# Keys, queries, values and sinks handed to a fused attention and two-layer MLP kernel in the layout of its groups

## The chip, the core and the metric

The kernel runs on one core of a Trainium2 chip. The metric is the device time of one execution in microseconds (us), as a median of several runs; lower is better. In the core, TensorE (PE) does the matrix products and the transposes into PSUM, ScalarE (ACT) and VectorE (DVE) read PSUM and do the elementwise work, GpSimd (POOL) does elementwise work on SBUF, and SyncE (SP) issues nearly all transfers. Each engine carries out its own instructions in a fixed order and waits on semaphores for the others.

## What is computed

Attention with two batches, eight heads, 768 positions and 64 channels per head, in which a query sees the first `n_sink` (4) keys and a window of 128 keys; then, on the 1536 x 512 result, two MLP layers. All weights come as 64-bit floats.

```python
scores = scale * np.matmul(q, k.transpose(0, 1, 3, 2))
keep = is_sink | in_window
scores = np.where(keep, scores, -1000000000.0)
a = np.exp(scores - np.max(scores, axis=-1, keepdims=True))
a = a / (np.sum(a, axis=-1, keepdims=True) + 1e-09)
attn = np.matmul(a, v)
...
g = x @ w_gate
y = (g * (1.0 / (1.0 + np.exp(-g))) * (x @ w_val)) @ w_out
h = y @ w_in
out = (np.maximum(h, 0.0) + alpha * np.minimum(h, 0.0)) @ w_out2
```

## The kernel before

The attention is cut into 24 groups. A group is one batch, one pair of heads (`hp`, of four) and 256 queries (two blocks of 128, from block `i0` on). The first eight groups have `i0 == 0`; they have no separate sink keys. The sixteen others (`i0` 2 or 4) see one key block before their own two and 32 sink keys; they come in pairs of neighbours, and the second of a pair (`before` is set) takes its first key block from the first one.

A score product contracts over the 64 channels of a head, so keys and queries must lie with channels on the partitions: two heads of 64 channels fill the 128 partitions. The inputs have positions on the rows. Therefore `load` (line 172) brings keys (`kr`) and queries (`qr`) with positions on the partitions, in runs of one head's 64 channels (256 bytes). `prep` (line 214) turns them: four transposes on TensorE into one PSUM tile `ps_k` (line 230) and a copy of it on ScalarE into the tile `th` (line 233 or 235); for the first of a pair one more transpose and copy (lines 225 and 226); for the second of a pair a copy on GpSimd (line 222); and for both a copy of the sink keys on GpSimd (line 219), which `sink_keys` (line 371) made by one transpose and one copy for each batch (lines 373 and 374). `load_v` brings values (`vr`), and for `i0 == 2` the sink values (`vsr`, line 209), four small transfers into a tile that GpSimd set to zero once (line 138).

`attention` (line 387) is the pipeline: in turn x it does the scores of group x, the values of group x - 3, the flips of group x - 2, the norm of group x, the prep of group x + 2, and it issues the loads of group x + 3 and the values of group x + 1. `scores` makes four score tiles `ps_s` (line 266), DVE adds the mask and takes the row's maximum (line 272, for sink groups after a merge in line 270), ACT takes the exponential with the row sum (line 276). `norm` makes the reciprocals `rinv` on DVE and scales on POOL. `flip` transposes the probabilities (line 321) and brings them to SBUF as `pt` (ACT in line 325 for the first eight groups, DVE in line 327 for the others). `values` makes `xp` (lines 352 and 357), and `put` splits it into a high part `xh` (ACT, line 869) and a low part `xl` (DVE, line 870).

Beside it the weights are streamed: a slice `w_raw` of 512 KB is loaded (lines 567 and 569), ACT makes `w_m` from it (line 585), DVE does three bit operations (lines 601, 604 and 607), ACT rounds to `wh` (line 615) and DVE makes the rest `wl` (line 621). The first 12 slices serve the first step (unit 0) of the MLP for all three passes of 512 positions, and they fill the 12 places that there are. After eight groups the attention is interleaved with the unit for the first pass, after sixteen with that for the second: each `yield` of the pipeline adds to `cost` (440 of it for each prep, 3,600 for the other parts of a group), and whenever `cost` has reached `WEAVE` = 2300 one step of the MLP is put in, and one step of a weight's conversion. What `cost` was gathered in the first eight groups is spent right after them.

The order on DVE is that of the code. On the other engines and queues a scheduler orders the instructions, by its own estimate of times. All PSUM tiles come from one pool of eight (`ps`).

Of the kernel before, what the change touches and what calls it, by code (L numbers as in the profile page):

```python
# [44 lines left out]
KW = P + SINK  # L45
DOWN = float(2.0**-112)
# [84 lines left out]
def attention_pools(nc, tc, ctx, g):  # L131
    for nm, bufs in (("raw_p", 2), ("tr_p", 3), ("pr_p", 3), ("pt_p", 2), ("st_p", 4)):
        setattr(g, nm, ctx.enter_context(tc.tile_pool(name=nm, bufs=bufs)))
    g.nb = g.const.tile([P, B * H * NQ], F32, name="nb")
    g.wsum = g.const.tile([P, NW], F32, name="wsum")
    g.kst = [g.const.tile([P, NPAIR * SINK], F32, name="kst") for _ in range(B)]
    g.vsr = g.const.tile([4 * SINK, NPAIR, NG, 2 * D], F32, name="vsr")
    nc.gpsimd.memset(g.vsr, 0.0)


class Group:
    def __init__(self, nc, g, q, k, v, b, hp, i0, put, cs, blk):
        self.nc, self.g, self.q, self.k, self.v = nc, g, q, k, v
# [7 lines left out]
        self.before = self.lead = None  # L151
        if self.sink:
            self.kpos = [0, P, P + KW]
            self.spos = 2 * P
            self.qpos = [P + 2 * KW, P + 3 * KW]
        else:
            self.kpos = [0, P]
            self.qpos = [2 * P, 3 * P]

    def wide(self, src, tag, bufs):  # L160
        t = self.g.raw_p.tile([P, NG, 4, D], F32, tag=tag, name=tag, bufs=bufs)
        for x in range(NG):
            self.nc.sync.dma_start(
                out=t[:, x], in_=src[self.b, self.h0:self.h0 + 4, x * P:(x + 1) * P, :].rearrange("h p d -> p h d")
            )
        return t

    def pair(self, t):
        e = 0 if self.lead is None else 2
        return t[:, :, e:e + 2].rearrange("p t e d -> p t (e d)")  # L170

    def load(self):
        nc, p = self.nc, self.g.raw_p
        b, h0, i0 = self.b, self.h0, self.i0
        if i0 == 0:
            if self.lead is None:
                self.raw = [self.wide(self.k, "kr", 2), self.wide(self.q, "qr", 2)]
            else:
                self.raw = self.lead.raw
            self.kr, self.qr = (self.pair(t) for t in self.raw)  # L180
            return
        n0 = 1 if self.before is not None else 0
        j0, nk = self.j0 + n0, self.nk - n0
        kr = p.tile([P, NG, 4, D], F32, tag="kr", name="kr", bufs=2)
        qr = p.tile([P, NG, 4, D], F32, tag="qr", name="qr", bufs=2)
        kr, qr = (x.rearrange("p t h d -> p (t h d)") for x in (kr, qr))
        kr = kr[:, :NK * 2 * D].rearrange("p (t e d) -> p t e d", e=2, d=D)
        qr = qr[:, :NG * 2 * D].rearrange("p (t e d) -> p t e d", e=2, d=D)
# [3 lines left out]
        self.qr, self.kr = (x.rearrange("p t e d -> p t (e d)") for x in (qr, kr))  # L192

    def load_v(self):
        nc, p = self.nc, self.g.raw_p
        b, h0, j0, nk = self.b, self.h0, self.j0, self.nk
        if self.i0 == 0:
            self.vt = self.wide(self.v, "vr", VB) if self.lead is None else self.lead.vt
            o = 0 if self.lead is None else 2
            self.vr = [[self.vt[:, t, o + e] for e in range(2)] for t in range(nk)]  # L200
            return
        vr = p.tile([P, NG, 4, D], F32, tag="vr", name="vr", bufs=VB).rearrange("p t h d -> p (t h d)")
        vr = vr[:, :NK * 2 * D].rearrange("p (t e d) -> p t e d", e=2, d=D)
        for e in range(2):
            nc.sync.dma_start(out=vr[:, :nk, e], in_=self.v[b, h0 + e, j0 * P:(j0 + nk) * P, :].rearrange("(t p) d -> p t d", p=P))
            if self.i0 == NG:
                for t in range(NG):
                    r = (2 * t + e) * SINK
                    nc.sync.dma_start(
                        out=self.g.vsr[r:r + SINK, self.hp, t, e * D:(e + 1) * D], in_=self.v[b, h0 + e, 0:SINK, :]  # L210
                    )
        self.vr = [[vr[:, t, e] for e in range(2)] for t in range(nk)]

    def prep(self):
        nc, g = self.nc, self.g
        self.th = th = g.tr_p.tile([P, P + 4 * KW], F32, tag="th", name="th")
        if self.sink:
            hp = self.hp
            nc.gpsimd.tensor_copy(th[:, self.spos:self.spos + SINK], g.kst[self.b][:, hp * SINK:(hp + 1) * SINK])
            if self.before is not None:  # L220
                o = self.before.kpos[2]
                nc.gpsimd.tensor_copy(th[:, 0:P], self.before.th[:, o:o + P])
            else:
                ps = g.ps_t.tile([P, 512], F32, tag="ps", name="ps_k0")
                nc.tensor.transpose(ps[:, 0:P], self.kr[:, 0], g.ident)
                nc.scalar.activation(th[:, 0:P], ps[:, 0:P], AF.Copy)
        ps = g.ps_t.tile([P, 512], F32, tag="ps", name="ps_k")
        k0 = self.nk - 2
        for x, src in enumerate([self.kr[:, k0], self.kr[:, k0 + 1], self.qr[:, 0], self.qr[:, 1]]):
            nc.tensor.transpose(ps[:, x * P:(x + 1) * P], src, g.ident)  # L230
        if self.sink:
            dst = th[:, P:].rearrange("p (x w) -> p x w", x=4)[:, :, 0:P]
            nc.scalar.activation(dst, ps.rearrange("p (x w) -> p x w", x=4), AF.Copy)
        else:
            nc.scalar.activation(th[:, 0:4 * P], ps, AF.Copy)
        yield 440
# [100 lines left out]
    def values(self):  # L337
# [17 lines left out]
        if self.sink:  # L355
            for t in range(n):
                nc.tensor.matmul(
                    xp[:, t * P:(t + 1) * P], g.vsr[:, self.hp, t], self.pts, start=False, stop=(t == n - 1), skip_group_check=True
                )
        self.put(xp[:, :n * P], self.hp, self.cs)  # L360
        yield 700


def sink_load(nc, g, k, b):
    g.ksr = g.raw_p.tile([NPAIR * SINK, 2 * D], F32, tag="ksr", name="ksr", bufs=1)
    kv = k[b].rearrange("(hp e) s d -> e hp s d", e=2)
    for e in range(2):
        nc.sync.dma_start(out=g.ksr[:, e * D:(e + 1) * D], in_=kv[e, :, 0:SINK, :])


def sink_keys(nc, g, b):
# [5 lines left out]
def attention(groups, begin):  # L377
# [15 lines left out]
    for x in range(n + LAG + 1):  # L393
# [20 lines left out]
        if x in (2, 4):  # L414
            begin[2](x // 2 - 1)
# [551 lines left out]
```

## Time and profile before

| | us |
|---|---|
| median of 3 runs | 687.81 |
| the runs | 687.81, 689.86, 687.18 |
| profiled execution, first to last instruction (span) | 685.5 |
| PE busy with matmuls, in the span | 658.3 |
| DVE busy | 408.5 |
| ACT busy | 303.8 |
| POOL busy | 44.9 |

The profiled execution has no time of its own other than its span; the runs' median is 2.3 us above it, for what lies before the first and after the last instruction. Busy times are sums over the whole span, and stages differ much: up to 189.56 us the attention is under way, alone for the first eight groups and then with MLP steps between, and the rest of the span is MLP alone. Matmuls are pipelined: the duration of one is longer than the distance to the next, so the cost of a few in a row is read from the distance.

### The profile page before, as it was taken

To read this page: it belongs to the slowest core of one execution; us is meant where nothing else is said; L and a number is where in the kernel's file an instruction comes from. 1 tells how busy PE (TensorE), PEld (TensorE's weight loads), DVE (VectorE), ACT (ScalarE), POOL (GpSimd) and SP (SyncE) were. 2 spreads that over 40 slices of the span, in tenths; PEclk is the share of its full clock that TensorE was granted. 3 is DMA by queue.
4 is the path that set the end of the run, shared out by engine and by line. 5 is a ranking of instruction groups with operands and counts; after the bars stand their busy time and mean duration, and the time that the engine had idled before them with its cause. 6 is when DMAs were issued, how large, how long until landed. Compare 5 with 4: busy or idle time off the path is not lost.

```text
span 685.5 us, 8954 instructions
## 1 busy us (share of the span) xinstructions
PE 658.3 (96%) x3195; PEld 527.1 (77%) x3195; DVE 408.5 (60%) x925; ACT 303.8 (44%) x688; POOL 44.9 (7%) x82
## 2 busy tenths in 40 slices
PE   5789999999899999999999999999999999999996
PEld 2557767777688888888888888888888888888885
DVE  5588789666389941379533589528833844334432
ACT  4796756766366612164322455436612432113320
POOL 3352013311000000000000000000000000000000
PEclk9999999999999999999999999999999999999999
DMA  8585355311046520033300043302500000000111
GB/s 161 136 211 159 104 159 118 88 34 29 1 139 191 166 89 0 1 123 126 121 0 1 5 143 120 102 1 64 171 11 0 1 0 1 0 1 1 61 62 66
DMA packets 76276, 50.87 MB, mean 74 GB/s; under 512 B 50624, under 2 KB 71104, under 8 KB 76224
## 3 DMA queue, kind: packets, MB, share of 16 engines
q1 hardware_dynamic: 73872, 50.22, 25.7%
q8 instruction: 27, 0.44, 0.3%
q10 hardware_dynamic: 2352, 0.01, 0.2%
q14 instruction: 25, 0.20, 0.1%
HBM read 47.07 MB, written 3.15 MB: 73 GB/s over the span
## 4 chain that ended last, share of the span: by engine, by line
PE 84%; DVE 3%; ACT 2%; issue 1%; DVEq 0%; ACTq 0%
PE ph L678 6%; PE ph L679 6%; PE pf L802 6%; PE pf L803 6%; PE pf L801 6%; PE ph L677 6%; PE po L746 4%; PE po L747 4%; PE po L745 4%; PE pv L677 4%; PE pg L677 4%; PE pg L678 4%; PE pg L679 4%; PE pv L679 4%; PE pv L678 4%; PE xp L352 2%
## 5 line engine op out<-in xcount | busy, mean ns | idle before, releaser
L690 ACT ACTIVATE hh<-hid 128x512 fp32r<-128x512 f32 x84 | 53.0, 631 | 65.3 <-DVE hid L729 36.0
L691 DVE TENSOR_TENSOR hl<-hid,hh 128x512 fp32r<-128x512 f32 x84 | 57.8, 689 | 37.1 <-ACT hh L690 37.0
L677 PE MATMUL ph<-yh,wh 128*128 128x512 f32 x192 | 74.8, 390 | 0.0
L678 PE MATMUL ph<-yl,wh 128*128 128x512 f32 x192 | 74.7, 389 | 0.0
L679 PE MATMUL ph<-yh,wl 128*128 128x512 f32 x192 | 74.7, 389 | 0.0
L802 PE MATMUL pf<-wl,hh 128*128 128x512 f32 x192 | 74.7, 389 | 0.0
L801 PE MATMUL pf<-wh,hh 128*128 128x512 f32 x192 | 74.7, 389 | 0.0
L783 ACT ACTIVATE neg<-ph,sal 128x512 f32<-128x512 f32 x48 | 33.0, 687 | 93.4 <-PE ph L679 93.4
L803 PE MATMUL pf<-wh,hl 128*128 128x512 f32 x192 | 72.1, 389 | 0.0
L615 ACT ACTIVATE wh<-w_m 128x512 fp32r<-128x512 f32 x68 | 42.7, 632 | 56.8 <-DVE w_m L607 16.5
L621 DVE TENSOR_TENSOR wl<-w_m,wh 128x512 fp32r<-128x512 f32 x68 | 46.6, 689 | 26.9 <-ACT wh L615 26.8
L785 DVE SCALAR_TENSOR_TENSOR hid<-ph,sig,neg 128x512 f32<-128x512 f32 x48 | 36.0, 749 | 38.4 <-ACT neg L783 38.0
L746 PE MATMUL po<-hh,wl 128*128 128x512 f32 x144 | 56.3, 392 | 1.1 <-DVE wl L621 1.1
L677 PE MATMUL pg<-xh,wh 128*128 128x512 f32 x144 | 56.8, 396 | 0.2 <-ACT pr L276 0.2
L677 PE MATMUL pv<-xh,wh 128*128 128x512 f32 x144 | 56.6, 393 | 0.0
L745 PE MATMUL po<-hh,wh 128*128 128x512 f32 x144 | 56.2, 397 | 0.4 <-ACT pts L335 0.2
L678 PE MATMUL pg<-xl,wh 128*128 128x512 f32 x144 | 56.2, 390 | 0.0
L679 PE MATMUL pg<-xh,wl 128*128 128x512 f32 x144 | 56.1, 390 | 0.0
L679 PE MATMUL pv<-xh,wl 128*128 128x512 f32 x144 | 56.1, 390 | 0.0
L678 PE MATMUL pv<-xl,wh 128*128 128x512 f32 x144 | 56.1, 390 | 0.0
L808 DVE TENSOR_TENSOR acc<-pf,acc 128x512 f32<-128x512 f32 x36 | 23.2, 685 | 52.0 <-PE pf L803 52.0
L747 PE MATMUL po<-hl,wh 128*128 128x512 f32 x144 | 53.1, 390 | 0.0
(122 smaller groups left out, 1200.5 us busy)
## 6 DMA issues: line engine op xcount, KB each, us to landing
w_raw<-in_moe_w_out SPq DMA_DIRECT2D x28, 512.0 KB, 3.3
w_raw<-in_moe_w_in SPq DMA_DIRECT2D x16, 512.0 KB, 3.7
w_raw<-in_moe_w_gate SPq DMA_DIRECT2D x12, 512.0 KB, 3.7
w_raw<-in_moe_w_val SPq DMA_DIRECT2D x12, 512.0 KB, 3.8
vr<-in_v SPq DMA_DIRECT2D x32, 96.0 KB, 2.2
out<-acc SPq DMA_DIRECT2D x12, 256.0 KB, 2.2
qr<-in_q SPq DMA_DIRECT2D x32, 64.0 KB, 2.3
kr<-in_k SPq DMA_DIRECT2D x16, 96.0 KB, 2.4
```

The source lines that it names most:

```text
L621: self.nc.vector.tensor_tensor(out=wl, in0=m, in1=wh, op=ALU.subtract)
L677: nc.tensor.matmul(ps, wh[:, c], xh[:, kk], start=(kk == 0), stop=False)
L678: nc.tensor.matmul(ps, wh[:, c], xl[:, kk], start=False, stop=False)
L679: nc.tensor.matmul(ps, wl[:, c], xh[:, kk], start=False, stop=(kk == KD - 1))
L690: nc.scalar.activation(hh, hid, AF.Copy)
L691: nc.vector.tensor_tensor(out=hl, in0=hid, in1=hh, op=ALU.subtract)
L745: nc.tensor.matmul(ps, wh[:, mc], hh, start=(x == 0), stop=False)
L746: nc.tensor.matmul(ps, wl[:, mc], hh, start=False, stop=False)
L747: nc.tensor.matmul(ps, wh[:, mc], hl, start=False, stop=(x == CHUNK - 1))
L801: nc.tensor.matmul(ps, hh[:, ts], wh, start=(x == 0), stop=False)
L802: nc.tensor.matmul(ps, hh[:, ts], wl, start=False, stop=False)
L803: nc.tensor.matmul(ps, hl[:, ts], wh, start=False, stop=(x == CHUNK - 1))
```

## The change

The host hands over five more arrays: `qk0` and `qk1` (for each group its keys, its sink keys and its queries, by channel, in just the columns of `th`), `v0` and `v1` (for each group its values, by position, two heads side by side) and `vs` (for each pair of heads the sink values, with the zeros). A group's `load` is now one transfer straight into `th` (256 KB for the first eight groups, 336 KB for the others), `load_v` one transfer (128 KB or 192 KB), and `vsr` one of 128 KB. `prep`, `sink_load` and `sink_keys` are gone with their transposes, copies and the GpSimd copies, and so is the zeroing of `vsr`. `th` has 4 buffers instead of 3; `vr` has 3 as before, but each now serves one group, also in the first eight, where it served two. Since `prep` yields no more, a group adds 3,600 to `cost` instead of 4,040, and a group has one `yield` less.

```diff
-    for nm, bufs in (("raw_p", 2), ("tr_p", 3), ("pr_p", 3), ("pt_p", 2), ("st_p", 4)):
+    for nm, bufs in (("raw_p", VB), ("tr_p", TB), ("pr_p", 3), ("pt_p", 2), ("st_p", 4)):
...
-    g.vsr = g.const.tile([4 * SINK, NPAIR, NG, 2 * D], F32, name="vsr")
-    nc.gpsimd.memset(g.vsr, 0.0)
+    g.vsr = g.const.tile([P, NPAIR, NG * 2 * D], F32, name="vsr")
...
     def load(self):
...
-        for e in range(2):
-            nc.sync.dma_start(out=kr[:, n0:self.nk, e], in_=self.k[b, h0 + e, j0 * P:(j0 + nk) * P, :].rearrange("(t p) d -> p t d", p=P))
-            nc.sync.dma_start(out=qr[:, :, e], in_=self.q[b, h0 + e, i0 * P:(i0 + NG) * P, :].rearrange("(t p) d -> p t d", p=P))
...
+        self.th = self.g.tr_p.tile([P, QOFF + NG * P], F32, tag="th", name="th")
+        self.nc.sync.dma_start(out=self.th[:, :self.qk_src.shape[1]], in_=self.qk_src)
...
     def load_v(self):
...
+        vr = self.g.raw_p.tile([P, NK * 2 * D], F32, tag="vr", name="vr")
+        nc.sync.dma_start(out=vr[:, :self.nk * 2 * D], in_=self.v_src)
+        if self.i0 == NG:
+            nc.sync.dma_start(out=self.g.vsr[:, self.hp], in_=self.vs_src)
...
-    def prep(self):
...
-        for x, src in enumerate([self.kr[:, k0], self.kr[:, k0 + 1], self.qr[:, 0], self.qr[:, 1]]):
-            nc.tensor.transpose(ps[:, x * P:(x + 1) * P], src, g.ident)
...
-        yield 440
...
-def sink_keys(nc, g, b):
-    ps = g.ps_t.tile([P, 512], F32, tag="ps", name="ps_ks")
-    nc.tensor.transpose(ps[:, :P], g.ksr, g.ident)
-    nc.scalar.activation(g.kst[b], ps[:, :P], AF.Copy)
...
-        if x + 2 < n:
-            for c in groups[x + 2].prep():
-                yield c, None
         stage("load", x + 3)
         stage("load_v", x + 1)
-        if x in (2, 4):
-            begin[2](x // 2 - 1)
...
+        for i in (NG, 2 * NG):
+            for hp in range(NPAIR):
+                kk, qq = kt[b, hp], qt[b, hp]
+                qk1.append(np.concatenate(
+                    [kk[:, cols[i - 1]], kk[:, cols[i]], kk[:, :SINK], kk[:, cols[i + 1]], qq[:, i * P:(i + 2) * P]], 1
+                ))
+                v1.append(rows(b, hp, i - 1, NK))
```

On TensorE, in the stretch of attention groups without MLP steps between (from about 107 to 127 us), one turn of the pipeline stood so before (`ps_k` are the transposes of keys and queries, `ps_p` those of probabilities, `ps_s` scores, `xp` values):

```order
L352 MATMUL xp<-pt,vr 64x256 x2
L352 MATMUL xp<-pt,vr 64x128 x4
L357 MATMUL xp<-pts,vsr 128x128 x2
L321 MATMUL ps_p<-ident,pr 128x128 x4
L334 MATMUL ps_p_1539<-ident,sk 128x128
L225 MATMUL ps_k_1550<-ident,kr 128x128
L230 MATMUL ps_k<-ident,kr 128x128 x2
L230 MATMUL ps_k<-ident,qr 128x128 x2
L266 MATMUL ps_s<-th 128x288 x4
```

and so now:

```order
L288 MATMUL xp<-pt,vr 64x256 x2
L288 MATMUL xp<-pt,vr 64x128 x4
L293 MATMUL xp<-pts,vsr 128x128 x2
L257 MATMUL ps_p<-ident,pr 128x128 x4
L270 MATMUL ps_p_1352<-ident,sk 128x128
L202 MATMUL ps_s<-th 128x288 x4
```

Four transposes, or five in the first group of a pair, are gone from the turn, and the scores stand right behind the flips.

On ScalarE, at the start (the first four exponentials, `pr`, are those of group 0, the next four those of group 1; `w_m` waits for a weight slice), these stood before:

```order
L235 ACT_TABLE_LOAD
L235 ACTIVATE th<-ps_k 128x512 x2
L276 ACTIVATE pr,ssum<-ps_s,nb 128x128 x2
L276 ACTIVATE pr,ssum<-ps_s,nb 128x256 x2
L276 ACTIVATE pr,ssum<-ps_s,nb 128x128 x2
L276 ACTIVATE pr,ssum<-ps_s,nb 128x256 x2
L235 ACTIVATE th<-ps_k 128x512 x2
L276 ACTIVATE pr,ssum<-ps_s,nb 128x128 x2
L585 ACTIVATE w_m,wsum<-w_raw 128x512
```

and now:

```order
L212 ACT_TABLE_LOAD
L212 ACTIVATE pr,ssum<-ps_s,nb 128x128 x2
L500 ACTIVATE w_m,wsum<-w_raw 128x512
L212 ACTIVATE pr,ssum<-ps_s,nb 128x256 x2
L500 ACTIVATE w_m,wsum<-w_raw 128x512
L212 ACTIVATE pr,ssum<-ps_s,nb 128x128 x2
L212 ACTIVATE pr,ssum<-ps_s,nb 128x256 x2
L261 ACTIVATE pt<-ps_p 128x2x128
```

The copies to `th` are gone, and the first two weight slices are taken up among the exponentials of group 0, where before the first one came among those of group 2.

On ScalarE, in the first unit of the MLP (`sg` is the gate's activation, which needs another function table than the exponential), these stood before:

```order
L721 ACTIVATE sg<-pg 128x512
L585 ACTIVATE w_m,wsum<-w_raw 128x512
L869 ACTIVATE xh<-xp 128x256
L615 ACTIVATE wh<-w_m 128x512
L276 ACT_TABLE_LOAD
L276 ACTIVATE pr,ssum<-ps_s,nb 128x160 x2
L721 ACT_TABLE_LOAD
L721 ACTIVATE sg<-pg 128x512
L276 ACT_TABLE_LOAD
```

and now:

```order
L212 ACT_TABLE_LOAD
L212 ACTIVATE pr,ssum<-ps_s,nb 128x160 x2
L636 ACT_TABLE_LOAD
L636 ACTIVATE sg<-pg 128x512
L212 ACT_TABLE_LOAD
L212 ACTIVATE pr,ssum<-ps_s,nb 128x160 x2
L778 ACTIVATE xh<-xp 128x256
L605 ACTIVATE hh<-hid 128x512
L636 ACT_TABLE_LOAD
L636 ACTIVATE sg<-pg 128x512
```

The unit's four `sg` are now split by exponentials in two places instead of one: from the first `sg` to the next exponentials behind the last one there are six table loads, where there were four.

## Rows read from the trace of the kernel before

**Rows 1.** Page, busy time of each engine, share of the span, instructions
```profile
PE 658.3 (96%) x3195; PEld 527.1 (77%) x3195; DVE 408.5 (60%) x925; ACT 303.8 (44%) x688; POOL 44.9 (7%) x82
```

**Rows 2.** Stretches (us): busy us of each engine (instructions), granted clock, DMA share, GB/s
```profile
0.00:10.53 10.53, 3.54 (x14) 1.99 (x16) 4.72 (x30) 2.37 (x3) 2.31 (x10) 1.00 0.80 120
10.53:16.40 5.87, 4.39 (x26) 2.63 (x26) 3.43 (x21) 4.51 (x18) 2.11 (x3) 1.00 0.91 214
16.40:44.17 27.77, 23.23 (x169) 15.87 (x165) 18.17 (x77) 23.28 (x84) 10.44 (x17) 0.94 0.68 168
44.17:55.02 10.85, 9.22 (x57) 6.09 (x56) 10.37 (x39) 9.49 (x33) 4.62 (x7) 1.00 0.83 204
55.02:93.15 38.13, 35.90 (x167) 26.03 (x166) 30.47 (x72) 24.92 (x56) 3.45 (x6) 1.00 0.46 134
93.15:106.95 13.80, 13.26 (x90) 9.44 (x90) 11.25 (x41) 9.01 (x30) 4.31 (x7) 1.00 0.52 136
106.95:127.02 20.07, 18.89 (x158) 14.98 (x159) 18.70 (x80) 12.37 (x51) 8.33 (x17) 1.00 0.49 111
127.02:189.56 62.54, 60.08 (x365) 45.01 (x364) 35.14 (x114) 35.84 (x92) 9.34 (x16) 1.00 0.14 31
189.56:685.50 495.94, 489.75 (x2161) 405.08 (x2160) 276.30 (x461) 182.03 (x324) 0.00 (x0) 1.00 0.19 61
```

**Rows 3.** Chain that ended last, in order of time: start, us, what
```profile
92.49 0.61 DVE wl L621
...
93.15 0.50 PE po L746
...
113.82 0.44 PE ps_k L230 x4
```

**Rows 4.** Groups by line: shapes, count, busy us, mean ns, idle before
```profile
L230 PE MATMUL ps_k<-ident,kr 128*128 128x128 f32 x48 | 10.6, 305 | 6.1 <-DMA kr<-in_k 5.6 <-ACT pr L276 0.3 <-ACT pt L325 0.2
```

**Rows 5.** Timeline of the start, DVE: start, us, instruction, idle before it
```profile
5.43 0.15 DVE L80 CAST wd_lo<-wd_raw 128x1 f32<-128x1 uint32 x1 [1.36 <-DMA wd_raw<-in_window]
...
10.53 0.30 DVE L272 CUSTOM_DVE_ANT_0 ps_s<-ps_s,mask 128x128 f32<-128x128 f32 x1 [0.64 <-PE ps_s L266]
```

**Rows 6.** Waits of DVE from 16.40 to 44.17: us, times, longest
```profile
DVE rinv L292 <- ACT pr L276: 4.5, 2, 2.7
DVE xl L870 <- ACT xh L869: 4.2, 3, 2.1
```

**Rows 7.** Stretches, tile ps_k alone: PE, PEld, ACT busy (instructions), clock, DMA
```profile
10.53:16.40 5.87, 1.60 (x8) 1.08 (x8) 1.09 (x2) 1.00 0.91 214
16.40:44.17 27.77, 4.36 (x25) 3.21 (x25) 4.15 (x7) 0.94 0.68 168
55.02:93.15 38.13, 1.31 (x9) 1.10 (x9) 1.35 (x3) 1.00 0.46 134
93.15:106.95 13.80, 1.31 (x9) 1.05 (x9) 1.48 (x3) 1.00 0.52 136
106.95:127.02 20.07, 2.89 (x21) 2.47 (x22) 2.77 (x6) 1.00 0.49 111
127.02:189.56 62.54, 2.34 (x17) 1.77 (x15) 2.84 (x6) 1.00 0.14 31
```

**Rows 8.** Timeline of ACT from 17 us on: taking up the first weight slice
```profile
18.49 0.66 ACT L585 ACTIVATE w_m<-w_raw 128x512 f32<-128x512 f32 x1 [0.89 <-DMA w_raw<-in_moe_w_gate]
```

**Rows 9.** Timelines in the first unit: a table load (ACT), a wait (DVE)
```profile
79.21 1.28 ACT L276 ACT_TABLE_LOAD   x1
...
82.56 0.69 DVE L621 TENSOR_TENSOR wl<-w_m,wh 128x512 fp32r<-128x512 f32 x1 [3.33 <-ACT wh L615]
```

**Rows 10.** Timeline from 24.99 us on, PE: before, in and after a long stop
```profile
25.00 0.87 PE L352 MATMUL xp<-pt,vr 128*64 128x256 f32 x8 [0.34 <-ACT pt L325]
...
29.49 0.30 PE L373 MATMUL ps_ks<-ident,ksr 128*128 128x128 f32 x1 [2.38 <-DMA ksr<-in_k]
...
30.57 1.49 PE L352 MATMUL xp<-pt,vr 128*64 128x256 f32 x8
```

More of the change, by code (lines that the diff above doesn't have):

```diff
@@ L158, in __init__ @@
             self.qpos = [2 * P, 3 * P]
[L160 to L170, printed above, removed]
@@ L194, in load_v @@
-    def load_v(self):
[L195 to L212, printed above, removed]
@@ L357, in values @@
                 nc.tensor.matmul(
-                    xp[:, t * P:(t + 1) * P], g.vsr[:, self.hp, t], self.pts, start=False, stop=(t == n - 1), skip_group_check=True
+                    xp[:, t * P:(t + 1) * P], g.vsr[:, self.hp, t * 2 * D:(t + 1) * 2 * D], self.pts, start=False, stop=(t == n - 1), skip_group_check=True
                 )
@@ L389, in attention @@
     begin[1]()
-    for x in range(2):
-        for c in groups[x].prep():
-            yield c, None
     for x in range(n + LAG + 1):
@@ L836, in moe, with fast @@
     return m1, Moe2(nc, g, st, 3 * NF1, ys, out, halves)
-def fast(nc, tc, ctx, g, n_sink, window, alpha, q, k, v, w_gate, w_val, w_out, x2_in, x2_out, out):
+def fast(nc, tc, ctx, g, n_sink, window, alpha, qk, vp, vs, w_gate, w_val, w_out, x2_in, x2_out, out):
     g.x_p = ctx.enter_context(tc.tile_pool(name="x_p", bufs=2 * NPASS))
@@ L874, in fast @@
         groups = [
-            Group(nc, g, q, k, v, blk // 3, hp, NG * (blk % 3), put(n, half), BLKS[half], blk)
+            Group(nc, g, qk, vp, vs, blk // 3, hp, NG * (blk % 3), put(n, half), BLKS[half], blk)
             for n, pair in enumerate(ORDER) for hp in range(NPAIR) for half, blk in enumerate(pair)
         ]
-        for x, y in zip(groups, groups[1:]):
-            if x.i0 == NG and y.i0 == 2 * NG and (x.b, x.hp) == (y.b, y.hp):
-                y.before = x
         groups[:2 * NPAIR] = groups[0:2 * NPAIR:2] + groups[1:2 * NPAIR:2]
-        for x in range(0, 2 * NPAIR, 2):
-            groups[x + 1].lead = groups[x]
         per = len(groups) // NPASS
@@ L886, in fast @@
         done = cost = 0
-        for c, grp in attention(groups, (begin_a, begin_b, begin_c)):
+        for c, grp in attention(groups, (begin_a, begin_b)):
             cost += c
@@ L926, in general, with build @@
             mix(nc, g, st, *moe(nc, g, st, xs, out, [[p * T]]))
-def build(nc, tc, q, k, v, n_sink, window, w_gate, w_val, w_out, x2_in, x2_out, alpha, out):
+def build(nc, tc, q, k, v, n_sink, window, w_gate, w_val, w_out, x2_in, x2_out, alpha, qk0, qk1, v0, v1, vs, out):
     with ExitStack() as ctx:
@@ L935, in build, with packed, by_channel, by_token @@
         setup(nc, tc, ctx, g)
-        args = (q, k, v, w_gate, w_val, w_out, x2_in, x2_out, out)
+        args = (w_gate, w_val, w_out, x2_in, x2_out, out)
         with ExitStack() as inner:
-            fast(nc, tc, inner, g, n_sink, window, alpha, *args)
+            fast(nc, tc, inner, g, n_sink, window, alpha, (qk0, qk1), (v0, v1), vs, *args)
         flag = nc.values_load(g.flag[0:1, 0:1], min_val=0, max_val=1)
         with tc.If(flag > 0):
-            general(nc, tc, g, *args)
+            general(nc, tc, g, q, k, v, *args)
 _INS = ["q", "k", "v", "n_sink", "window", "moe_w_gate", "moe_w_val", "moe_w_out", "moe2_w_in", "moe2_w_out", "moe2_alpha"]
+def packed(q, k, v):
+    import numpy as np
+    def by_channel(a):
+        return a.reshape(B, NPAIR, 2, S, D).transpose(0, 1, 2, 4, 3).reshape(B, NPAIR, P, S)
+    def by_token(a):
+        return a.reshape(B, NPAIR, 2, S, D).transpose(0, 1, 3, 2, 4).reshape(B, NPAIR, S, 2 * D)
+    qt, kt, vt = by_channel(q), by_channel(k), by_token(v)
+    cols = [slice(i * P, (i + 1) * P) for i in range(NQ)]
+    def rows(b, hp, j0, nk):
+        return np.concatenate([vt[b, hp, cols[j]] for j in range(j0, j0 + nk)], 1)
+    qk0, qk1, v0, v1, vs = [], [], [], [], []
+    for b in range(B):
+        for hp in range(NPAIR):
+            kk, qq = kt[b, hp], qt[b, hp]
+            qk0.append(np.concatenate([kk[:, :2 * P], qq[:, :2 * P]], 1))
+            v0.append(rows(b, hp, 0, 2))
+            z = np.zeros((NG, 2, SINK, NG, 2, D), v.dtype)
+            for t in range(NG):
+                for e in range(2):
+                    z[t, e, :, t, e] = v[b, 2 * hp + e, :SINK]
+            vs.append(z.reshape(P, NG * 2 * D))
+        for i in (NG, 2 * NG):
+            for hp in range(NPAIR):
+                kk, qq = kt[b, hp], qt[b, hp]
+                qk1.append(np.concatenate(
+                    [kk[:, cols[i - 1]], kk[:, cols[i]], kk[:, :SINK], kk[:, cols[i + 1]], qq[:, i * P:(i + 2) * P]], 1
+                ))
+                v1.append(rows(b, hp, i - 1, NK))
+    return {nm: np.stack(x) for nm, x in (("qk0", qk0), ("qk1", qk1), ("v0", v0), ("v1", v1), ("vs", vs))}
 def kernel(**inputs):
```

69 lines of the change are left out of this document (14 added, 55 removed).

## The prediction, made before the changed kernel had run

> **What bounds the kernel now.** The first view is the busy time of the whole span [rows 1]: matmuls on PE cover 658.3 of 685.5 us. Read alone, this says that PE is the bound and that each matmul taken away is won. Two further views correct it.
>
> The second view cuts the span where the work changes [rows 2]. From 189.56 us on only the MLP is left, PE has 489.75 of 495.94 us, and the change has no instruction there. In the last attention stretch (127.02 to 189.56) PE has 60.08 of 62.54 us, DVE only 35.14: PE is the bound. In the stretch of plain groups (106.95 to 127.02) PE has 18.89 and DVE 18.70 of 20.07: two engines near their limit. Between 44.17 and 55.02 DVE has 10.37 of 10.85. Before that, where the first eight groups run, ACT is the fullest (4.51 of 5.87, then 23.28 of 27.77), and at the very start nobody is full.
>
> The third view, the chain that ended last, followed back, agrees [rows 3]: its pieces are PE's from 93.15 us on, mostly; just before, it comes from DVE and ACT, through the conversion of a weight slice. So before 93 us a matmul less on PE is worth nothing by itself; what counts there is what ACT and DVE do.
>
> **The change part by part.** The 24 groups lose four transposes each, eight of them (the first ones of pairs) a fifth, and the two calls of `sink_keys` one each: 106. One lasts 305 ns on average [rows 4], but four in a row take 0.44 us of PE's time [rows 3], so 0.11 us each. ACT loses a copy for each, too; how many fall where is in the windows of the tile `ps_k` [rows 7]. I go stretch by stretch; all signs are against 685.5 us.
>
> *Start, to the first mask work on scores at 10.53.* DVE waited 0.64 us there for PE's scores, which waited for transposes and a copy [rows 5]; `th` now comes straight from memory, so this goes. Next late are the masks, which stand ahead on DVE and began at 5.43, after 1.36 us of waiting for the window's value [rows 5]. With fewer and longer runs in the queues this small transfer may come earlier, up to those 1.36. So between -0.6 and -2.0; I take -1.0, nearer to the end that needs no assumption.
>
> *First eight groups, 10.53 to 44.17.* DVE waits for ACT in 4.5 + 4.2 us of the stretch [rows 6], since the reciprocal of a group needs its four exponentials and the next group's mask work stands behind it. ACT drops nine copies of 1.09 + 4.15 = 5.2 us [rows 7]. If ACT is in the way all the time, -5.2. It is busy 83% (27.79 of 33.64) [rows 2], so 4.3 us of it count. Against that, ACT now takes up two weight slices within group 0, and the exponentials of group 1, all copies and DVE's turn queue behind them. Up to and with the second slice, the queue on SP has five `th` of 256 KB, three `vr` of 128 KB and two slices of 512 KB: 2,688 KB or 2.75 MB, 12.9 us at the 214 GB/s of the busiest early stretch [rows 2]. (The fifth `th` waits on SP until group 0's scores free a buffer, and the second slice queues behind it; those scores need only the first `th`, so this is over long before.) From a first issue some 0.7 us in, that ends at 13.6, and the slice costs ACT about 0.8 us. The exponentials of group 1 stood at 13.6 before, so they are 0.8 us late: 4.3 - 0.8 gives **-3.5**. The ends are -5.2 and, if the transfers take longer, a loss (rival 3). The transfers of later groups hide behind this: 256 + 128 KB in some 4 us are under 100 GB/s beside the slices. `vr` now waits on SP for the values of three groups before, with the next `th` and slice queued behind; that `th` is needed three turns later, so 0, and up to a turn of some 4 us once if it were not.
>
> *44.17 to 55.02.* DVE bound, its work unchanged: 0. PE's transposes and ACT's copies are hidden by DVE here.
>
> *First MLP unit and after, 55.02 to 106.95.* Chain of ACT and DVE up to 93. ACT loses copies of 1.35 + 1.48 = 2.8 us [rows 7]. But the new order loads two more function tables, 1.28 us each [rows 9], 2.6 us, at a place where DVE had waited 3.33 us behind such loads [rows 9]. I take 0, with the ends -2.8 and +2.6.
>
> *Plain groups, 106.95 to 127.02.* PE loses 21 transposes, 2.3 us, but DVE has only 20.07 - 18.70 = 1.4 us to give before it is the bound itself. I take -1.2; ends -1.4 and 0.
>
> *Second unit, 127.02 to 189.56.* PE bound: 17 transposes less by the records, 17 x 0.11 = -1.9. A group brings 440 less of `cost`, so MLP steps move later by a fraction of one; the matmuls are the same. Ends -1.0 (some gaps there are waits for `pt`, which stay) and -2.3, the busy time [rows 7].
>
> *The rest.* 0. GpSimd's copies and the zeroing go too, but POOL is busy 44.9 us in all [rows 1]; 0.
>
> Sum: -1.0 - 3.5 - 1.2 - 1.9 = -7.6, a span of 677.9. The runs' median stands 2.3 us above the span of the profiled execution, so I expect a median of **680.2 us** (-1.1%). All the good ends give -13.7 (674.1), all the bad ones without rival 3 +1.0 (688.8).
>
> **The rivals.**
>
> *1. PE is the bound all the way.* Then all 106 transposes count: 11.7 us, 676.1. For it: PE's 96%, and 35.90 of 38.13 us in the first unit [rows 2]. Against it: the chain before 93 us, and the 6 us that PE is not busy in the first eight groups. [...]
>
> *2. The early gain is swallowed.* ACT's relief finds DVE or the pipeline's latency as the next limit, and the two table loads count in full: -0.6 + 2.6 - 1.2 - 1.9 = -1.1, that is 686.7, no difference that can be told. For it: DVE is nearly full from 44 us on, so whatever comes earlier must also find the slices converted earlier. Against it: DVE's waits for ACT [rows 6] are real idle time.
>
> *3. ACT stands before weights that have not landed* (slower). The first slice landed late before as well: ACT waited 0.89 us for it at 18.49 [rows 8]. If the transfers run at the 120 GB/s of the first stretch [rows 2], the 2.75 MB end at 0.7 + 22.9 = 23.6 us instead of 13.6, and ACT, with the exponentials of group 1 behind, waits 10 us longer than in the sum; the two slices that are then done save 1.7 later. 680.2 + 10.0 - 1.7 = 688.5. It decides from a second slice later than about 22 us on (then the early gain is gone); later still, it passes 691. Against it: those 120 GB/s came from runs of 256 bytes, and the new ones have 1 to 2.7 KB.
>
> *4. TensorE falls to its lower clock in the first groups*, since the transposes that kept it busy are gone. Before, after a stop of 2.38 us, the same eight value matmuls took 1.49 us instead of 0.87 [rows 10], and the granted clock of the stretch was 0.94 of 2.4 GHz [rows 2]. If all of PE's work in the first eight groups were slower by that ratio, 1.71: 27.6 us [rows 2] less the removed 6.0 [rows 7] is 21.7, times 1.71 is 37.0 against 33.6 that the stretch took: 3.4 us lost instead of 3.5 won, 687.1. Against it: the stop was for the sink keys' transfer, which goes. The Trainium skill ("TensorE: Matmul & The Clock Gate", Part 1: The HAM clock gate) says that the throttled clock is the default and that activity releases it, which speaks against taking matmuls away. The trace shows such a fall once.
>
> That the change would not do what it says is no rival: in the order of the new program no transpose into `ps_k` is left on PE, and each group has one transfer for `th`.
>
> **How the numbers follow.** The forecast gets 0.66, rival 1 0.15, rival 2 0.10, rival 3 0.06, rival 4 0.03. A difference of 0.5% (3.4 us, so under 684.4 or over 691.3) is about what a measurement of this kernel can tell from none. Faster are rival 1 and the forecast but for a twentieth of it (its bad ends go past 684.4): 0.15 + 0.63 = 0.78. Within it are that rest, rivals 2 and 4 and a third of rival 3: 0.18. Beyond it are the later landings of rival 3: 0.04. The range goes from 674.3, about the sum of the good ends, to 686.0, past the forecast's own bad ends but short of rivals 2 and 3, which leaves out less than 2 in 10.
>
> **What would show it.** Right: the first mask work on scores at about 9.5 us, the ninth group's at about 39.7 instead of 44.17, no change of length from there to the first unit, plain groups with DVE full, the last group's end some 7 us earlier, and the MLP's rest unchanged at 496 us. Wrong: ACT idle in front of the first two `w_m`, for longer than 1 us; a granted clock well under 1 before 40 us; a first unit that takes much more than 38 us, with ACT's table loads in its chain; or plain groups shorter than DVE's work.

## The result, and the profile of the changed kernel

The changed kernel takes 693.5 us (median; 693.1 to 694.5), the kernel before on the same chip 688.8. The ratio is 1.0078, with a 95% interval of 1.0060 to 1.0096: slower by 0.8%, where 680.2 us, faster, was forecast.

The page of the changed kernel says nothing of this. Its busy times, to be read beside [rows 1], all went down:

```profile
PE 657.8 (95%) x3089; PEld 520.7 (75%) x3089; DVE 408.0 (59%) x925; ACT 292.4 (42%) x656; POOL 36.9 (5%) x57
```

Matmuls fell by 106, as the diff says, and ScalarE by 32 instructions; yet the span grew from 685.5 to 691.5 us. A span that grows while every engine works less has new idle time in it, and the way to find it is to cut both traces at the same events. Each group has one reciprocal (`rinv`) on DVE. The cuts below are the eleventh, thirteenth and nineteenth group's reciprocals and the first gate matmul after attention. First the kernel before, then the changed one (stretch, its length, busy us of each engine with instructions, granted clock, DMA share, GB/s):

```profile
0.00:63.93 63.93, 48.59 (x297) 32.85 (x298) 45.29 (x187) 45.43 (x152) 20.88 (x38) 0.97 0.71 165
63.93:102.27 38.34, 36.81 (x187) 26.25 (x184) 28.88 (x69) 25.39 (x60) 4.81 (x8) 1.00 0.48 137
102.27:129.28 27.01, 25.29 (x204) 19.77 (x203) 24.90 (x102) 17.36 (x70) 10.18 (x21) 1.00 0.51 115
129.28:189.39 60.11, 57.65 (x353) 43.01 (x352) 33.01 (x107) 33.60 (x84) 9.04 (x15) 1.00 0.12 27
189.39:685.50 496.11, 489.92 (x2162) 405.24 (x2160) 276.47 (x461) 182.03 (x324) 0.00 (x0) 1.00 0.19 61
```

```profile
0.00:60.50 60.50, 46.00 (x244) 29.59 (x244) 44.76 (x188) 39.15 (x137) 17.13 (x29) 0.97 0.64 189
60.50:103.45 42.95, 39.40 (x174) 27.43 (x174) 28.92 (x69) 25.91 (x56) 2.98 (x4) 0.88 0.41 127
103.45:129.24 25.79, 23.01 (x178) 15.90 (x176) 24.48 (x102) 13.10 (x60) 8.41 (x12) 1.00 0.50 143
129.24:195.60 66.36, 59.44 (x340) 42.55 (x339) 32.20 (x105) 31.54 (x79) 8.40 (x12) 0.97 0.07 21
195.60:691.50 495.90, 489.91 (x2162) 405.26 (x2160) 277.69 (x462) 182.70 (x326) 0.00 (x0) 1.00 0.19 61
```

The differences are -3.4, +4.6, -1.2, +6.3 and -0.2 us. The third and the last are about what was forecast, and the first is 1.1 us short of its -4.5. The second and the fourth, the two stretches in which MLP steps are woven between the groups, lose 10.9 us.

**The first unit (60.50 to 103.45).** In it DVE stood still twice for long (DVE of the changed kernel: start, us, instruction, idle before it and what ended that):

```profile
68.29 0.69 DVE L644 TENSOR_TENSOR hid<-pv,sg 128x512 f32<-128x512 f32 x1
73.73 0.69 DVE L606 TENSOR_TENSOR hl<-hid,hh 128x512 fp32r<-128x512 f32 x1 [4.75 <-ACT hh L605]
...
102.05 1.29 DVE L263 TENSOR_TENSOR pt<-ps_p,tri 128x512 f32<-128x512 f32 x2 [5.44 <-PE ps_p L257]
```

For the first stop, see what ScalarE did meanwhile:

```profile
66.66 1.28 ACT L212 ACT_TABLE_LOAD   x1
...
68.83 1.28 ACT L636 ACT_TABLE_LOAD   x1
70.13 0.60 ACT L636 ACTIVATE sg<-pg 128x512 f32<-128x512 f32 x1
70.75 1.28 ACT L212 ACT_TABLE_LOAD   x1
...
73.06 0.64 ACT L605 ACTIVATE hh<-hid 128x512 fp32r<-128x512 f32 x1
```

`hid` was ready at 69.0, but its split `hh` stands on ScalarE behind a gate activation (`sg`), the second half of the next group's exponentials and a table load for each, since the two kinds alternate. DVE runs in its written order, so the conversions of the next weight slices behind `hl` wait too. In the chain of work that ended last, the stretch behind this stop is the conversion of one slice after another, by ScalarE and DVE in turn, and TensorE enters it only at 88.42 (start, us, what):

```profile
73.18 0.53 ACT hh L605
...
80.03 0.64 ACT wh L530
...
87.77 0.61 DVE pt L263
88.42 0.80 PE po L660
```

TensorE meanwhile stands before what DVE does late (its longest waits from 76 to 93 us are 1.7 us for `hid` and 1.4 us for `pt`), and its clock falls (stretches of 4 us, columns as above):

```profile
76.00:80.00 4.00, 3.87 (x18) 2.33 (x16) 3.20 (x7) 1.83 (x6) 0.00 (x0) 1.00 0.42 137
80.00:84.00 4.00, 1.96 (x6) 0.95 (x7) 3.35 (x6) 2.19 (x5) 0.00 (x0) 0.96 0.46 133
84.00:88.00 4.00, 3.04 (x5) 1.11 (x5) 3.49 (x7) 1.41 (x4) 0.00 (x0) 0.50 0.73 217
88.00:92.00 4.00, 3.58 (x8) 2.81 (x9) 3.97 (x7) 1.06 (x2) 0.00 (x0) 0.50 0.41 131
92.00:96.00 4.00, 4.00 (x24) 2.67 (x23) 3.93 (x17) 3.56 (x10) 1.58 (x2) 0.76 0.55 172
```

After 80 to 84, where PE was busy for 1.96 of 4 us, the granted clock is 0.50, the 1.2 GHz level, until about 94 us. The second stop, 5.44 us, is DVE waiting for transposes that stand on PE behind matmuls of the MLP; PE is busy all that time (4.00 of 4 us from 96 to 100), working off the MLP steps that came late.

**The last groups (129.24 to 195.60).** TensorE is the bound there, so its own idle time counts. The kernel before first, then the changed one (PE from 155 us on, all rows with idle time before them):

```profile
172.90 1.09 PE L352 MATMUL xp<-pt,vr 128*64 128x256 f32 x12 [0.35 <-DVE pt L327]
178.99 1.09 PE L352 MATMUL xp<-pt,vr 128*64 128x256 f32 x12 [1.05 <-DVE pt L327]
185.08 1.09 PE L352 MATMUL xp<-pt,vr 128*64 128x256 f32 x12 [1.05 <-DVE pt L327]
```

```profile
172.82 1.55 PE L288 MATMUL xp<-pt,vr 128*64 128x256 f32 x8 [3.56 <-issue]
181.20 0.87 PE L288 MATMUL xp<-pt,vr 128*64 128x256 f32 x8 [1.58 <-DVE pt L263]
188.16 0.87 PE L288 MATMUL xp<-pt,vr 128*64 128x256 f32 x8 [1.58 <-DVE pt L263]
```

A turn of the tail takes 6.96 us (181.20 to 188.16) instead of 6.09 (178.99 to 185.08). In the kernel before, the 12 `po` matmuls of an MLP step stand between a group's values and the next transposes; in the changed one they stand between the two parts of a group's values (`x8`, then the rest). In the last turns of both, nothing stands between a group's transposes and its values to cover the wait for `pt`. But in the changed kernel the earlier group's values now end right ahead of the transposes, so that their `xl` stands on DVE ahead of `pt` (DVE, the kernel before, then the changed one):

```profile
183.73 1.29 DVE L327 TENSOR_TENSOR pt<-ps_p,tri 128x512 f32<-128x512 f32 x2 [2.13 <-PE ps_p L321]
```

```profile
186.49 0.42 DVE L779 TENSOR_TENSOR xl<-xp,xh 128x256 fp32r<-128x256 f32 x1 [5.34 <-ACT xh L778]
186.83 1.28 DVE L263 TENSOR_TENSOR pt<-ps_p,tri 128x512 f32<-128x512 f32 x2
```

So PE waits 1.58 us instead of 1.05; the rest of the 0.87 us is PE's own time, with the values cut in two. At 169.3 no MLP matmul stood between transposes and values, where the kernel before still had three (0.35 us idle, first row above); DVE had `hid`, `hl` and `xl` ahead of `pt`, PE was idle for 3.56 us, and the eight matmuls behind that took 1.55 us instead of 0.87.

### The profile page after: what moved, and what is told of

Its sections match the earlier page's. It is cut to its first block, busy times and chain, and to the rows that moved or that the text cites. A ratio compares the mean times of both kernels' runs of the same rounds, so it can differ in the third digit from the quotient of the medians.

```text
span 691.5 us, 8567 instructions
## 1 busy us (share of the span) xinstructions
PE 657.8 (95%) x3089; PEld 520.7 (75%) x3089; DVE 408.0 (59%) x925; ACT 292.4 (42%) x656; POOL 36.9 (5%) x57
## 4 chain that ended last, share of the span: by engine, by line
PE 80%; DVE 5%; ACT 2%; issue 1%; ACTq 0%
PE ph L593 6%; PE ph L594 6%; PE pf L717 6%; PE pf L718 6%; PE pf L716 6%; PE ph L592 6%; PE po L660 5%; PE po L662 5%; PE po L661 5%; PE pg L592 4%; PE pg L593 4%; PE pg L594 4%; PE pv L592 4%; PE pv L594 4%; PE pv L593 4%; PE xp L288 2%
## 5 line engine op out<-in xcount | busy, mean ns | idle before, releaser
L660 PE MATMUL po<-hh,wh 128*128 128x512 f32 x144 | 57.7, 405 | 1.4 <-DVE pt L263 1.4
L202 PE MATMUL ps_s<-th 64*128 64x288 f32 (+2 forms) x192 | 42.0, 464 | 12.7 <-DMA th<-in_qk 5.4
```

The source lines that it names most:

```text
L660: nc.tensor.matmul(ps, wh[:, mc], hh, start=(x == 0), stop=False)
```

## The experiments

Three theories were set against each other. **W**: what costs the time is that key preparation no longer hands `yield 440` to the weave. **C**: TensorE's clock falls because the transposes that kept it busy are gone. **D**: the larger transfers cost it. All ratios are against the kernel before, run on the same chip.

**1. The step put back, with no work behind it.**

```diff
+    for x in range(2):
+        yield 440, None
     for x in range(n + LAG + 1):
...
+        if x + 2 < n:
+            yield 440, None
         stage("load", x + 3)
```

> The changed kernel, with the step of cost 440 that every group's key preparation used to hand to the weave put back at the same places (no work behind it), so that MLP steps and weight conversions stand in the order of the kernel before. Three theories. W (the weave): the loss comes only from the missing 440, by which MLP steps and weight conversions fall later between the groups; then this kernel keeps the 3.4 us that the changed kernel is ahead after the tenth group and some 1 us of the plain groups, and the last attention work ends 3 to 6 us before that of the kernel before: 0.990 to 0.995 of its time. C (the clock): TensorE, without the transposes, does not stay at its upper clock in the first unit; then nothing is won back: 1.005 to 1.010, and the granted clock of 80 to 100 us is again near 0.74. D (transfers): the whole loss comes from larger transfers and their queues, which are as in the changed kernel: 1.006 to 1.010.

Measured: 677.6 us, 0.9842 (0.9823 to 0.9861), more than W expected, 16 us better than the changed kernel. Its stretches, cut at the same events:

```profile
0.00:59.64 59.64, 45.14 (x239) 29.62 (x240) 44.77 (x188) 39.16 (x137) 17.10 (x29) 0.94 0.64 192
59.64:96.19 36.55, 35.65 (x179) 25.59 (x178) 28.89 (x69) 20.88 (x52) 3.71 (x4) 1.00 0.47 149
96.19:121.57 25.38, 22.56 (x175) 15.78 (x175) 24.34 (x103) 12.96 (x60) 8.39 (x12) 1.00 0.49 145
121.57:180.98 59.41, 56.48 (x340) 41.41 (x339) 32.32 (x105) 31.95 (x79) 8.39 (x12) 1.00 0.08 23
```

The first unit is 6.4 us shorter than in the changed kernel and has a clock of 1.00; the last groups are 7.0 us shorter. DVE's long stop is gone: the two gated products of a pair (`hid`) and their splits both stand ahead of the next scores' masks, and of the five table loads from 59.41 to 73.72 us two are left (58.55 and 72.38). The kernel before had four in this unit, so on ScalarE the order is not quite the one of before. The transfers are those of the changed kernel, and no transpose of keys or queries is there; so C and D, as causes of the loss, are out.

**2. The same edit alone, on the kernel before.** The loops over `prep()` run it to the end and hand nothing on:

```diff
             for c in groups[x + 2].prep():
-                yield c, None
+                pass
```

> The kernel before with its transposes, copies and transfers, whose key preparation hands no cost and no step to the weave (the weave of the changed kernel, alone). W: the changed kernel lost 3.6 us from its tenth to its twelfth group's reciprocal and 6 us after the last scores; the same edit alone should cost the kernel before 4 to 10 us: 1.006 to 1.015. C and D: the transposes and the transfers are as before, so 0.998 to 1.002.

Measured: 701.8 us, 1.0182 (1.0157 to 1.0206): 13.3 us lost, with all transposes and old transfers in place, and above W's own range. The changed kernel's waits are all there, first DVE, then PE:

```profile
78.20 0.69 DVE L691 TENSOR_TENSOR hl<-hid,hh 128x512 fp32r<-128x512 f32 x1 [3.08 <-ACT hh L690]
107.81 1.29 DVE L327 TENSOR_TENSOR pt<-ps_p,tri 128x512 f32<-128x512 f32 x2 [6.23 <-PE ps_p L321]
```

```profile
181.51 1.47 PE L352 MATMUL xp<-pt,vr 128*64 128x256 f32 x8 [3.14 <-issue]
190.05 0.87 PE L352 MATMUL xp<-pt,vr 128*64 128x256 f32 x8 [1.58 <-DVE pt L327]
```

By stretches, cut as above, the loss in the two traces is 2.1, 4.9, 0.8 and 7.3 us. The 2.1 fall in the first groups, where TensorE's stop before the sink keys lasts 4.01 us instead of 2.38 [rows 10]; the rest repeats what the changed kernel lost.

So the change is two changes: with the weave as it was, the new layout wins 10.9 us (688.5 to 677.6); without the step it wins 8.3 (701.8 to 693.5).

**3 and 4. The number of steps, and the place for one.** The step had a cost and a place: a point, between a group's normalisation and the next scores, where the weave may put one MLP step.

```diff
-WEAVE = 2300
+WEAVE = 2050
```

> The changed kernel with its weave threshold scaled to the cost of a group that is left, 2300 x 3600 / 4040 = 2050: as many MLP steps to a group as before, but one place less in a group where a step can stand. W: nearly as good as the step put back, 0.990 to 0.999. C and D: as the changed kernel, 1.005 to 1.010.

Measured: 684.1 us, 0.9935 (0.9919 to 0.9952). Then the place without the cost (as in run 1, but `yield 0, None`):

> The changed kernel with the place of the removed step put back (a point between a group's normalisation and the next group's scores where an MLP step may stand), but not its cost of 440. The theory so far: there are two losses. In the first unit steps are plenty and it is the number of places that limits them; the missing place lets only one of the two gated products of a pair stand ahead of the next scores, and its split waits on ScalarE behind exponentials. After the twelfth group it is the cost: fewer steps to a group, so more of them fall into the tail. Expected then: the twelfth to thirteenth group (reciprocals) as in the kernel with the step put back, 88.5 and 96.2 us, granted clock 1.00 at 80 to 100 us, but a tail of some 19 us instead of 13 after the last reciprocal: 684 to 688 us, 0.993 to 1.000. Rival, that only the number of steps to a group counts: then this is no better than the changed kernel, 1.005 to 1.010.

Measured: 684.8 us, 0.9959 (0.9943 to 0.9974), both inside the ranges expected for them. The two halves repair different stretches. With the cost alone, DVE still stops in the first unit (first fence), but the tail has no idle time on PE over 0.7 us. With the place alone, the thirteenth group's reciprocal comes at 95.76 and the clock stays at 1.00 from 60 to 140 us, but the tail is that of the changed kernel (second fence, PE):

```profile
73.42 0.69 DVE L606 TENSOR_TENSOR hl<-hid,hh 128x512 fp32r<-128x512 f32 x1 [4.75 <-ACT hh L605]
102.00 1.29 DVE L263 TENSOR_TENSOR pt<-ps_p,tri 128x512 f32<-128x512 f32 x2 [5.70 <-PE ps_p L257]
```

```profile
164.68 0.87 PE L288 MATMUL xp<-pt,vr 128*64 128x256 f32 x8 [3.54 <-issue]
173.21 0.87 PE L288 MATMUL xp<-pt,vr 128*64 128x256 f32 x8 [1.58 <-DVE pt L263]
```

The halves won 9.4 and 8.7 us alone, and 15.9 together.

**5. Only TensorE kept busy, the weave as changed.** Four transposes for each group from the third on (88 in all), from `th`, into PSUM; nobody reads them.

```diff
+        if x + 2 < n:
+            groups[x + 2].spin()
...
+        for y in range(4):
+            nc.tensor.transpose(ps[:, y * P:(y + 1) * P], self.th[:, y * P:(y + 1) * P], g.ident)
```

> The changed kernel, with four transposes to a group put back on TensorE from the keys as handed over, whose result nobody reads (no copy of it), where the key preparation stood; the weave stays as changed. C: the clock of the first unit comes back, and with it the time: 0.995 to 1.002. W: still late, and with some 2 us more of matmuls in the stretch that TensorE bounds: 1.006 to 1.014. D: 1.006 to 1.012.

Measured: 693.6 us, 1.0075 (1.0052 to 1.0097), and DVE stops for 4.76 us before `hl` again, with a clock of 0.74 from 80 to 100 us, as in the changed kernel. The fall of the clock follows the stop; more transposes do not prevent it.

**6 and 7. Where the gain is.** Run 1 with the transposes put back at their places (a fifth for the first of a pair), then also with ScalarE's copies, into a tile that nobody reads:

> The changed kernel with the step put back, and with its transposes on TensorE too (four to each group, a fifth for the first one of each pair, from the keys as handed over; nobody reads the result): the part of the gain that is TensorE's. By the sum of the prediction, plain groups 1.2 and second unit 1.9 us come back: 678 to 682 us, 0.986 to 0.991. If TensorE were the bound all the way: 11 us, 0.997 to 1.002.

> As the run with the transposes put back, and ScalarE's copies of them with them (into a tile that nobody reads), so that of the change only the new transfers and the missing waits on them are left, and the sink keys' part. By the prediction's sum ScalarE's copies are worth 3.5 us of the first eight groups: 682 to 686 us, 0.991 to 0.997. If the gain were the transfers': 677 to 680 us, 0.983 to 0.988. If it is all work on the engines: 0.998 to 1.002.

Measured: 680.8 us, 0.9898 (0.9879 to 0.9917), and 680.5 us, 0.9896 (0.9878 to 0.9915). So TensorE's part is 3.2 us by the medians (3.9 by the ratios), near the 3.1 of the sum; in the traces the plain groups and the last ones each get 1.6 us longer. The copies cost nothing: in run 7 ScalarE has 15.7 us more to do in the first 200 us than in run 6 (131.0 against 115.3), and the eleventh group's reciprocal comes at 58.90 against 58.50. Run 7 lies between the two ranges set for it, nearer to the one for the transfers; since run 6 without the copies is no better, what is missing to run 1 is PE's.

Of some 10.9 us, then, 3 to 4 come from PE, and 7.5 (688.0 to 680.5) stay with all that run 7 does not put back: the new transfers, the scores that need not wait for a transpose and a copy of their keys, the sink keys' part, and GpSimd's copies and zeroing. In the trace of run 7, 5.0 us of it lie before the eleventh reciprocal. The other 2.1 lie in the first unit, where ScalarE has two table loads instead of four; by the trace that part goes with the order and not with the transfers, and no run parts the two.

**8. The start.** Run 1 with `slopes` called after the nineteenth group:

```diff
     def begin_b():
         masks(nc, g)
-        slopes(nc, g, alpha)
...
+        if x == 18:
+            begin[2]()
```

> The changed kernel with the step put back, and the small transfer of alpha with its four small operations on DVE moved from the start to the nineteenth group. In the changed kernel the issue of the second weight slice on SP waited 3.1 us for that transfer, and ScalarE then 1.3 us for the slice (0.7 with the step put back). Theory: the start term was missed for this; then the first two groups' reciprocals (13.65 and 16.73 us) come 0.5 to 1.5 us earlier, and of it 0 to 1.5 us reaches the end: 0.982 to 0.985, against 0.984. Rival, that the slice is late for the bytes ahead of it: no change at the start.

Measured: 674.6 us, 0.9809 (0.9794 to 0.9825), more than expected, and not by the cause that was put forward. Only DVE's four operations moved; the transfer's issue stayed at the start of ScalarE's queue, and SP's issue of the second weight slice still waited for it:

```profile
SPq L490 <- DMA alpha<-in_moe_alpha: 3.1, 1, 3.1
```

What changed is DVE: the first mask work on scores began at 9.76 instead of 10.67 us, since the four operations, and 0.20 us of waiting for `alpha` before them, no longer stand ahead of it. And on ScalarE the late slice now stands behind group 1's exponentials and not ahead of them (run 1, then this run):

```profile
14.13 0.67 ACT L504 ACTIVATE w_m<-w_raw 128x512 f32<-128x512 f32 x1 [0.72 <-DMA w_raw<-in_moe_w_gate]
```

```profile
14.24 0.67 ACT L506 ACTIVATE w_m<-w_raw 128x512 f32<-128x512 f32 x1
```

The slice is taken up at the same time, but the second group's reciprocal comes at 14.51 instead of 16.73. How much each of the two is worth, this one run does not part.

**9 and 10. Which transfers.** The kernel before, with the second batch's sink keys loaded behind the first group into their own buffer (`bufs=2`); and the kernel before with the values and sink values alone in the new layout:

> The kernel before, with the second batch's sink keys loaded behind the first group into a buffer of their own, so that the stop of 2.38 us on TensorE before their transpose goes (the second weight slice is issued behind the fourth group's keys for it). The run with transposes and copies put back kept the whole lead of the first eight groups, so the lead comes from transfers. Theory S: nearly half of it is this stop. Then the sixth group's reciprocal comes 1.5 to 2.5 us earlier than 35.57, and the end 0 to 2.5: 0.996 to 1.000. Theory T: the stop hides another wait, and the lead is in the transfers' volume of small runs: no change, 0.999 to 1.002.

> The kernel before, with the values and sink values alone handed over in the groups' layout (one transfer each, no setting to zero); keys, queries, transposes, copies and the weave as before. Theory S: the values' transfers take their share of a queue that is full from 10 to 20 us (DMA share 0.96), so the wait of 0.89 us for the first weight slice shrinks, and the third group's reciprocal comes 0.5 to 1 us earlier than 20.66; the 15 sink value transfers that stood ahead of the second batch's sink keys become 3, so their stop shrinks as well, and the sixth group comes 1.5 to 3 us earlier: 0.995 to 0.999. Theory T, that keys and queries carry the gain: 0.999 to 1.002.

Measured: 686.7 us, 0.9973 (0.9962 to 0.9984), and 685.3 us, 0.9960 (0.9946 to 0.9974). In both, the stop of 2.38 us [rows 10] is gone and the sixth group's reciprocal comes early (34.95 and 33.61 instead of 35.57): by 0.6 us in run 9, where 1.5 to 2.5 were expected, and by 2.0 in run 10, as expected. The third group's did not come earlier in run 10, as expected, but later (21.59 instead of 20.66). Both ratios lie inside the ranges of theory S, whose account of the third group did not hold. With the sink keys loaded early the weights are late: ScalarE's wait for the first slice [rows 8] doubles and a second one comes (first fence), while the values' new layout more than halves it, with a second one of 0.39 (second fence):

```profile
19.52 0.66 ACT L586 ACTIVATE w_m<-w_raw 128x512 f32<-128x512 f32 x1 [1.80 <-DMA w_raw<-in_moe_w_gate]
25.39 0.67 ACT L586 ACTIVATE w_m<-w_raw 128x512 f32<-128x512 f32 x1 [1.19 <-DMA w_raw<-in_moe_w_gate]
```

```profile
17.58 0.67 ACT L575 ACTIVATE w_m<-w_raw 128x512 f32<-128x512 f32 x1 [0.36 <-DMA w_raw<-in_moe_w_gate]
```

The two overlap (both remove the stop). Of run 7's 7.5 us some 4.4 (7.5 - 3.1) remain by subtraction for the keys, the queries and the sink keys, among them the 2.1 of the first unit; that part was not run alone, and its cause stays open.

**11. A version that beats both.** Run 8 with the threshold at 2150:

> The version with the step put back and alpha's operations late, with a threshold of 2150 in place of 2300, so that some 7% more MLP steps stand between the groups. If the tail after the last scores still loses for want of steps done earlier, 671 to 674 us (0.976 to 0.980); if the step put back has already met what the stretch can take, the plain groups, which DVE bounds, get a step more and nothing is won: 674 to 678 us (0.980 to 0.986).

Measured: 672.6 us, 0.9778 (0.9757 to 0.9799), as expected if steps were still wanting; 2.2% under the kernel before and 3.0% under the changed one, with the change's layout, the step put back, and `slopes` late.

## Why the prediction was wrong

**The step that failed** is one sentence on the second unit: "A group brings 440 less of `cost`, so MLP steps move later by a fraction of one; the matmuls are the same." It saw the edit and priced it at nothing. The matmuls are indeed the same, but the order was the price. Run 2 puts 13.3 us on that edit alone, more than the 7.6 of all the gains in the sum. In the changed kernel the loss fell into just the two stretches for which 0 and -1.9 stood: +4.6 and +6.3 (in run 2, 4.9 and 7.3 of the loss). The order of the new program already showed a part of it, the two more table loads on ScalarE. They were seen and given a bound of +2.6; what was not followed is what stands in a row behind them on DVE, the conversions of the next slices, and that TensorE stops for what DVE then does late. None of the rivals had the weave in it, so the range had no place for 693.5. Its upper end was set too low besides: 686.0 is called past the forecast's own bad ends, but these add up to 688.8 a few lines earlier.

**The sum without that step** comes out near. Run 1 is the change nearly as the sum imagined it: 677.6 us against 680.2, inside the range. By stretches (traces, against the kernel before; the cuts are those of the first section, a little off those of the forecast):

| | forecast | run 1 |
|---|---|---|
| start and first groups, to the eleventh reciprocal | -4.5 | -4.3 |
| first unit, to the thirteenth | 0 | -1.8 |
| plain groups, to the nineteenth | -1.2 | -1.6 |
| last groups | -1.9 | -0.7 |
| the rest | 0 | -0.1 |

The plain groups came out as argued: DVE has 24.34 of 25.38 us there and is the bound. The first unit is 1.8 shorter, with two table loads of 1.28 us fewer.

**Right size, wrong cause.** The 3.5 us of the first groups were put on ScalarE's copies, since DVE's waits named ScalarE [rows 6]. Run 7 has the copies and keeps the gain, and in it the two waits of [rows 6], from 16.40 to 44.17 us, are 2.3 and 2.4 us instead of 4.5 and 4.2. That -4.5 came so near to -4.3 is luck. ScalarE was the last to finish, but what made it late lay elsewhere: runs 9 and 10 show the stop before the sink keys [rows 10] and the late slices [rows 8] as parts of it. Besides, the scores of the third group had waited 1.48 us (to 15.88) for the copy `th` itself to be done, a wait that goes with the copies' place in the chain and not with their time on ScalarE; what it was worth is not shown. A wait "for ScalarE" names who came last, not why. The argument "busy 83%" was no proof either: TensorE was as full in that stretch (23.23 of 27.77 us, ScalarE 23.28) [rows 2].

**The start was missed.** -1.0 was forecast; the first mask work came at 10.92 instead of 10.53 us. The 0.64 us of waiting for scores did go, but the window's value landed later than before, not earlier (its cast at 6.24 instead of 5.43 [rows 5]), and DVE waited another 0.21 us for `alpha`. The second group's reciprocal came 2.0 us late, because its exponentials stood behind the second slice on ScalarE, which waited for it (first line). SP had issued that slice only at 10.33, after waiting for `alpha`, a transfer in another queue that the prediction had not looked at (second line):

```profile
14.98 0.67 ACT L500 ACTIVATE w_m<-w_raw 128x512 f32<-128x512 f32 x1 [1.31 <-DMA w_raw<-in_moe_w_gate]
```

```profile
SPq L484 <- DMA alpha<-in_moe_alpha: 3.1, 1, 3.1
```

**The rivals.** Rival 1 (PE the bound all the way) fell with run 6: 104 of the 106 transposes are worth 3.2 us, not 11.7. Rival 2 (the early gain swallowed) fell with run 1: 4.3 us were won by the eleventh reciprocal and kept. Rival 3 had the right place, but the wait was 1.3 us, not 10, and was made up by the third group (20.22 against 20.66). Rival 4 was right that the clock could fall, but had neither the stretch nor the cause: it fell in the first unit, after a stop and not for want of transposes (run 5). Two signs that the prediction named for being wrong came: ScalarE idle for more than 1 us before one of the first two `w_m` (1.31), and a first unit much longer than 38 us (42.95). The table loads stand in the row ahead of `hh`, as shown; the chain itself can be followed back only to the exponentials at 72.53, right behind the third of them.

## What to carry to other kernels

Where a planner weaves work by a cost budget and at places where a step may stand, removed work takes its cost and its place with it; put both back, or tune the budget anew, before the change is judged, and run the weave's edit alone, since it can be worth more than the work removed. Compare the two programs' orders for what now stands behind a waiting instruction on each engine that runs in order, not for the count of instructions. And before a wait is credited to the engine that it names, look at what made that engine late.

## What the runs showed of the hardware

- A stop on TensorE costs more than its length: after 80 to 84 us, with 1.96 of 4 us busy, the granted clock was 0.50 until about 94, and the same 12 value matmuls took 1.76 us at 92.56 instead of the 1.09 at 103.44. The Trainium skill ("TensorE: Matmul & The Clock Gate", Part 1: The HAM clock gate) has the throttled clock as the default, released by activity; the trace agrees, but run 5 shows that a little more activity elsewhere does not help where the stop itself stays.
- A switch between exponential and gate activation cost 1.30 us from the end of one to the start of the next (68.83 to 70.13, the load 1.28 of it). The Trainium skill ("ScalarE: Activation LUTs", What ACT_TABLE_LOAD costs) gives 1283 ns for the load and 2.66 us with a drain; here the load agrees, no drain shows, and the measured 1.30 us decides.
- A transfer of 8 KB in runs of 4 bytes (`alpha`) took 8.4 us to land in run 1 and held up, by 3.1 us, the issue of a weight slice on another engine's queue. The trace names the wait; why the two are tied to each other, no run here shows.
